# A chunked attention followed by a top-2 mixture of experts: tiles of 96 slots per pair of experts, the tokens beyond them in a list of each expert

## The chip, the cores and the metric

The kernel runs on one core of one Trainium2 chip, in one launch. A core has a matrix engine (TensorE, PE in the profile), three engines for vector work (VectorE or DVE, ScalarE or ACT, GpSimd or POOL) and SyncE (SP), which here only issues transfers. Each engine works through its own instructions in order; semaphores make one wait for another. Data lie in SBUF (128 partitions), matmul results in PSUM banks, inputs and outputs in DRAM. The metric is the device time of one execution in microseconds; smaller is better.

## The reference, cut to what matters

```python
def _attn_ref(q, k, v, mem_k, mem_v):              # (4, 8, 768, 64); chunks of 32, 16 to the left, 8 to the right, 8 memory rows
    ...
        a = np.exp(scores)
        a = a / (np.sum(a, axis=-1, keepdims=True) + 1e-09)
        out[:, :, c_start:c_end] = np.matmul(a, v_full)

def _moe_ref(x, w_gate, w_noise, noise, w1, w2):   # N=3072 tokens, D=512, E=8 experts, F=1024
    noisy_logits = x @ w_gate + np.log1p(np.exp(x @ w_noise)) * noise
    top2 = np.argpartition(-noisy_logits, 2, axis=1)[:, :2]
    ...
            h = np.maximum(x[mask] @ w1[e], 0.0)
            out[mask] += top2_w[mask, k, None] * (h @ w2[e])
```

Each token goes to the two experts with the largest noisy logits; their two outputs are added with the softmax of those two logits as weights. Inputs are drawn once, so the counts are the same in every run. Counted from that draw, a pair of experts has 87 to 135 tokens (28 pairs, 3072 tokens); one pair has more than 128, 23 have more than 96; the tokens beyond 96 of the seven pairs of an expert are 51 to 136.

## The kernel before, in words

The kernel has two stages. The first, to about 131 us, is the attention: 12 steps written out by hand (`ORDERS`), with the router's work in between. It writes the attention's rows to the DRAM tile `xd`, and routes each token to its **pair** of experts: `pcode` holds a code for each of the `NP` = 28 pairs, `ohp` is the one-hot of a token's pair, `rank` its place in it, `cum` the counts so far, `facts` five facts of a token besides (its row, its weights). One-hots of the rank (`oh_l`, L336) times these facts give, by matmul, `listed`: for each pair and each of 128 slots, which token stands there. From it come `main_src` (rows of `xd` to gather), `main_dst` (rows of the output) and `main_w` (weights).

The second stage runs the experts. The weights (float32 in DRAM, 2 MB for each of an expert's two layers) are cast to bf16 on their way into `w_all`, which holds all 8 experts, by transfers that POOL issues (L77, L79, L89, L91: `load_layer`, `load_part`). A pair's 128 rows are gathered by an indirect DMA of POOL (L896, `gather_x`), turned to columns by a DMA transpose of SP (L921) or, for the first six, by PE (L916), and lie in `xTs`, in blocks of 6 or 8 pairs. Twenty steps go through the blocks, an expert with 2, 3 or 4 of its pairs in each: `mm1` (L939) multiplies w1 by the columns into the banks `p_h`, ACT and DVE apply relu into `h` (L925, L927), `mm2` (L950) multiplies by w2 into `p_y`, of which there are two banks. A pair's first expert writes `y` (ACT, L954), its second adds to it (DVE, L956), and POOL puts the rows into the output (L902). The second layer of a step runs after the first layer of the next, so relu is not waited for. Tokens of a pair beyond 128 go to extra tiles: up to 32 of the first such tile through the spare tile in column groups of the array (L1122, L1142), with weights loaded for it anew (L1078, L1079); more by a branch at the end (L1220).

What sets the order: PE, ACT, DVE and SP are ordered by hand in the first stage, PE at the stage's start and otherwise by the scheduler's estimate; POOL's transfers are marked to keep the program's order (`pin`), but the scheduler's order can differ from the text's, as shown below. All transfers that POOL issues go into one queue, `q0`, SP's into `q1`.

## Time and profile before

| | |
|---|---|
| runs | 347.87, 348.86, 343.81 us; median 347.87 |
| span of the profiled execution | 344.8 us |
| PE busy | 291.0 us (84%) in 3332 matmuls |
| DVE, ACT, POOL busy | 157.4, 132.7, 150.9 us |
| transfers of POOL's queue | 40.51 MB, 60.9% of 16 DMA engines' span |
| transfers of SP's queue | 7.18 MB, 11.7% |

The profiled execution has no time of its own beside its span; the span lies inside the range of the runs, 3.1 us under their median. Busy times are sums over both stages, which have different limits, so they say little by themselves; the views below are read by stage. In the chain and in the timeline a row gives its start and its length in us, then engine, tile and line. `issue` is time in which an engine waited for nothing that the profile shows. In the list of transfers the last number is the median time from issue to landing.

### The profile page before, as it was taken

What the parts mean: (1) busy time and instruction counts of PE and PEld (TensorE: products, weight loads), DVE (VectorE), ACT (ScalarE), POOL (GpSimd) and SP (SyncE); (2) the same over time, 40 slices, a digit from 0 to 9 for tenths busy, and PEclk for the clock granted to TensorE, in tenths of its full rate; (3) what the DMA queues carried; (4) which work ended last, traced back from release to release, by engine and by line L of the source; (5) the groups of instructions that cost most, each with busy time, mean ns of one, the idle gap of its engine ahead of it and who ended that gap; (6) DMA issues with size and microseconds to landing.
All of it is one profiled execution on the core that took longest, in us unless ns stands there. A gap on an engine that the chain in (4) does not pass through costs nothing.

```text
span 344.8 us, 7971 instructions
## 1 busy us (share of the span) xinstructions
PE 291.0 (84%) x3332; PEld 192.8 (56%) x3332; DVE 157.4 (46%) x319; ACT 132.7 (38%) x220; POOL 150.9 (44%) x232
## 2 busy tenths in 40 slices
PE   0566889876778744999999999999999999999990
PEld 0465878765766633855544466664455775555550
DVE  4764657575579786311324166344310333312230
ACT  4656637553476310344231443213243222233300
POOL 4679678944019156821821555231670132201142
PEclk9969898888799655999999999999999999999997
DMA  7999959996804912897999999991289991100011
GB/s 123 212 211 194 222 104 209 189 179 114 161 2 72 201 33 62 134 205 195 172 194 207 267 138 249 199 167 54 92 167 189 204 209 59 55 2 2 27 73 58
DMA packets 41288, 48.32 MB, mean 140 GB/s; under 512 B 16000, under 2 KB 31362, under 8 KB 41244
## 3 DMA queue, kind: packets, MB, share of 16 engines
q0 software_dynamic: 23712, 40.51, 60.9%
q1 hardware_dynamic: 16988, 7.18, 11.7%
q8 instruction: 28, 0.46, 0.5%
q14 instruction: 16, 0.13, 0.1%
q10 hardware_dynamic: 544, 0.03, 0.1%
HBM read 64.88 MB, written 10.55 MB: 219 GB/s over the span
## 4 chain that ended last, share of the span: by engine, by line
PE 66%; DMA 5%; DVE 5%; issue 2%; ACT 2%; POOL 0%; POOLq 0%; SPq 0%; DVEq 0%
PE p_h L939 29%; PE p_y L950 28%; DMA w_all<-mvn 4%; PE p_t L409 2%; PE ps_o L578 1%; PE p_v L438 1%; DMA xt<-xd,main_src 1%; PE p_p L558 1%; PE p_xt L916 1%; ACT w_all L413 1%; ACT pT L564 1%; PE ps_s L465 1%; PE p_x L600 1%; DVE w_all L591 1%; PE p_rank L303 0%
## 5 line engine op out<-in xcount | busy, mean ns | idle before, releaser
L939 PE MATMUL p_h<-xTt,w_all 128*128 128x256 bf16 (+3 forms) x672 | 101.9, 312 | 0.5 <-DVE xTt L917 0.5
L950 PE MATMUL p_y<-w_all,h 128*128 128x512 bf16 x440 | 98.2, 379 | 0.0
L939 PEld LDWEIGHTS <-w_all 128*128 128x128 bf16 x672 | 65.3, 99 | 35.5 <-issue 0.9
L927 ACT ACTIVATE h<-p_h 128x512 bf16<-128x512 f32 (+1 forms) x79 | 43.4, 550 | 88.9 <-PE p_h L939 78.0
L950 PEld LDWEIGHTS <-h 128*128 128x128 bf16 x440 | 42.9, 98 | 49.2
L902 POOL DMA_INDIRECT out_dram<-y,main_dst x27 | 27.0, 998 | 82.4 <-DVE y L956 74.0
L925 DVE TENSOR_SCALAR h<-p_h 128x512 bf16<-128x512 f32 (+1 forms) x47 | 29.6, 631 | 69.0 <-PE p_h L939 63.4
L389 POOL COPY w_all<-w_all 128x512 bf16<-128x512 bf16 (+1 forms) x59 | 42.3, 785 | 17.1 <-PE p_t L409 11.8
L956 DVE SCALAR_TENSOR_TENSOR y<-p_y,main_w,y 128x512 f32<-128x512 f32 x27 | 20.3, 751 | 43.4 <-PE p_y L950 42.4
L896 POOL DMA_INDIRECT xt<-xd,main_src x28 | 27.4, 978 | 28.9 <-DMA xTt<-xt 12.1
L954 ACT ACTIVATE y<-p_y,main_w 128x512 f32<-128x512 f32 x28 | 19.2, 687 | 36.5 <-PE p_y L950 35.5
L409 PE MATMUL p_t<-identf,w_all 128*128 128x128 f32 x120 | 22.5, 337 | 0.4 <-ACT pT L564 0.4
L591 DVE TENSOR_TENSOR w_all<-ps_o,rs 128x512 bf16<-128x512 f32 x24 | 15.7, 683 | 7.3 <-PE ps_o L578 6.5
L409 PEld LDWEIGHTS p_t<-identf,w_all 128*128 128x128 f32 x120 | 17.9, 178 | 1.4 <-issue 1.0
L438 PE MATMUL p_v<-identf,w_all 128*128 128x128 f32 x96 | 15.9, 304 | 2.5 <-ACT w_all L413 1.8
L564 ACT COPY pT<-p_p 128x1024 bf16<-128x1024 bf16 x11 | 11.1, 1012 | 11.7 <-PE p_p L558 11.5
L478 DVE TENSOR_REDUCE mx<-ps_s 128x16 f32<-128x1024 f32 x12 | 14.7, 1223 | 1.8 <-PE ps_s L465 1.5
L480 DVE TENSOR_TENSOR w_all<-ps_s,mx 128x1024 f32<-128x1024 f32 x12 | 14.7, 1225 | 0.8
L551 ACT ACTIVATE pb<-w_all 128x1024 bf16<-128x1024 f32 x12 | 12.7, 1062 | 6.0 <-DVE w_all L480 6.0
L413 ACT COPY w_all<-p_v 128x512 f32<-128x512 f32 x21 | 11.9, 588 | 8.0 <-PE p_v L438 8.0
L578 PE MATMUL ps_o<-w_all,pT 64*32 64x64 bf16 x768 | 9.3, 201 | 6.6 <-DMA w_all<-mvn 4.4
L405 PE MATMUL p_t<-identb,w_all 128*128 128x128 bf16 x48 | 4.6, 270 | 11.9 <-DVE w_all L389 11.9
(220 smaller groups left out, 294.3 us busy)
## 6 DMA issues: line engine op xcount, KB each, us to landing
w_all<-in_moe_w_dram POOLq DMA_DIRECT2D x16, 1024.0 KB, 11.8
w_all<-in_moe_w_dram POOLq DMA_DIRECT2D x8, 512.0 KB, 12.7
w_all<-in_k_dram POOLq DMA_DIRECT2D x4, 768.0 KB, 11.5
w_all<-in_q_dram POOLq DMA_DIRECT2D x4, 768.0 KB, 9.2
w_all<-in_v_dram POOLq DMA_DIRECT2D x4, 768.0 KB, 12.4
xd<-w_all SPq DMA_DIRECT2D x24, 128.0 KB
w_all<-mvn SPq DMA_DIRECT2D x24, 32.0 KB
xt<-xd,main_src POOLq DMA_INDIRECT x28, 10.9
```

The costliest lines, as they stand in the source:

```text
L389: i = eng.tensor_copy(to, x)
L409: nc.tensor.transpose(out=p_t[:, s, :], in_=m.bitcast(F32)[:, s * 128:(s + 1) * 128], identity=identf)
L438: nc.tensor.transpose(out=p_v[:, i, c, :], in_=vT[:, c, c0:c0 + 128], identity=identf)
L591: nc.vector.tensor_tensor(out=xrow[b % 2][:, 2 * tp + j, 0:Dm].rearrange("p (x d) -> p x d", x=H), in0=ps_o[:, j], in1=bc(rs[:, :, j], D), ...
L896: i = nc.gpsimd.indirect_dma_start(out=xts[key].bitcast(I32), out_offset=None, in_=xd, in_offset=bass.IndirectOffsetOnAxis(ap=ix, axis=0))
L902: i = nc.gpsimd.indirect_dma_start(out=out if rows is None else rows, out_offset=bass.IndirectOffsetOnAxis(ap=ix, axis=0), in_=y, in_offse ...
L925: nc.vector.tensor_scalar(out=out_, in0=in_, scalar1=0.0, scalar2=None, op0=Alu.max)
L927: nc.scalar.activation(out=out_, in_=in_, func=Act.Relu)
L939: nc.tensor.matmul(out=o, lhsT=w(kp * F + f * 128, 128), rhs=x[:, kp], start=(kp == 0), stop=(kp == KP - 1))
L950: nc.tensor.matmul(out=p, lhsT=h[:, (f * n + j) * 128:(f * n + j + 1) * 128], rhs=w(KP * F + f * Dm, Dm), start=(f == 0), stop=(f == FB - 1))
L954: nc.scalar.activation(out=y, in_=p, func=Act.Copy, scale=weight)
L956: nc.vector.scalar_tensor_tensor(out=y, in0=p, scalar=weight, in1=y, op0=Alu.mult, op1=Alu.add)
```

## The change

A pair's tile has `MT` = 96 slots. The pairs are numbered anew: pairs (i, i+1), (i, i+2) and (i, i+3), counted around, are numbers 3i, 3i+1, 3i+2 (`out_of(i)` for expert i, `in_of` for the other one); the four **opposite** pairs (i, i+4) are numbers 24 to 27. Experts run one after the other. An expert has three tiles out, three in, one opposite pair of 96, and a list of its own with 160 places (`RS`): the tokens beyond 96 of its seven pairs, up to 64 of each (`RU`).

For the first layer an opposite pair's 96 columns and the 160 listed ones stand side by side in `x3`. For the second, a tile has 128 rows again: 96 of a pair and 32 beside them, from the opposite pair (tiles out, `hO`) or from the list's first 96 places (tiles in, `hI`); the list's last 64 places (`hB`) run in two column groups of 64. What the 32 rows give is copied by a second instruction on `p_y` into a unit tile (L1043).

The listed tokens' facts are made by one-hots once more (`rest_onehots`, `rest_list`), written to the DRAM tile `tdr`, and read back by indirect DMAs, two for each expert (`rest_facts`); decoded on DVE (`rest_decode`), gathered (`rest_rows`) and turned (`turn_rest`). A listed token is in the lists of both its experts: the earlier stores its weighted result to the output (`put_rest`), the later reads that back (`get_prev`, into `pA` and `pB`), adds its own and stores the sum. The spare tile is gone; a pair beyond 160 or a list beyond 160 goes to the branch at the end (`overflow`).

`w_all` keeps 5 experts (`WR`), expert e in place e % 5; what is freed holds `xs`, `hO`, `hI`, `hB` and `x3`. Weights are loaded in whole layers.

```diff
+    WR = 5
-            pin(nc.gpsimd.dma_start(out=w1v[:, e], in_=moe_w1[e].rearrange("(kp p) f -> p kp f", p=128)))
+            pin(nc.gpsimd.dma_start(out=w1v[:, e % WR], in_=moe_w1[e].rearrange("(kp p) f -> p kp f", p=128)))
...
-            eng.tensor_tensor(out=self.oh_l, in0=bc(self.rr, 128), in1=io_l.unsqueeze(1).to_broadcast([128, n, 128]), op=Alu.is_equal)
+            eng.tensor_tensor(out=self.oh_l, in0=bc(self.rr, MT), in1=io_l[:, 0:MT].unsqueeze(1).to_broadcast([128, n, MT]), op=Alu.is_equal)
...
+    def mm2_tiles(e, ps, h, unit):
+        for k, g in enumerate(ps):
+            p = psY.tile([128, Dm], F32, name="p_y")
+            for f in range(FB):
+                nc.tensor.matmul(out=p, lhsT=h[:, f, k, :], rhs=w2(e, f), start=(f == 0), stop=(f == FB - 1))
...
+                y = ys[g] = yp.tile([128, Dm], F32, name="y")
+                nc.scalar.activation(out=y[0:MT], in_=p[0:MT], func=Act.Copy, scale=wt)
+                keep_unit(0, unit[32 * k:32 * k + 32], p)
...
+    def ins_(e):
+        unit = yrp.tile([128, Dm], F32, name="yr")
+        mm2_tiles(e, in_of(e), hI, unit)
+        p = psY.tile([128, Dm], F32, name="p_y")[:, 0:Dm // 2]
+        for f in range(FB):
+            for g in range(2):
+                nc.tensor.matmul(out=p[g * RU:(g + 1) * RU], lhsT=hB[:, f, :], rhs=w2(e, f, g * Dm // 2, Dm // 2),
+                                 start=(f == 0), stop=(f == FB - 1), tile_position=(0, g * RU))
...
+            pA, pB = prev.pop(e)
+            nc.vector.scalar_tensor_tensor(out=yB, in0=p, scalar=wB, in1=pB, op0=Alu.mult, op1=Alu.add)
+            nc.vector.scalar_tensor_tensor(out=unit[0:MT], in0=unit[0:MT], scalar=wA, in1=pA[0:MT], op0=Alu.mult, op1=Alu.add)
+        put_rest(yB, dB, outB, 2 * N)
+        put_rest(unit[0:MT], dA, out, N)
+
+    def get_prev(e):
...
+        get_rest(pA[0:MT], rest_of[e][4], out, N)
+        get_rest(pB, rest_of[e][5], outB, 2 * N)
...
+    def rest_list():
...
+            nc.tensor.matmul(out=p, lhsT=oh_t[:, g], rhs=vals_t[:, g], start=(g == 0), stop=(g == NG - 1))
+        nc.vector.tensor_copy(tsb[:, :, 0:NV], p.rearrange("p v c -> p c v"))
+        for h in range(2):
+            nc.sync.dma_start(out=tdr.rearrange("(s h c) v -> h s (c v)", h=2, c=NC2)[h],
+                              in_=tsb[h * RU:(h + 1) * RU].rearrange("p c v -> p (c v)"))
+
+    def rest_facts(e):
+        for b, n in ((0, MT), (1, 128)):
+            i = nc.gpsimd.indirect_dma_start(out=fr[0:n, b, e], out_offset=None, in_=tdr,
+                                             in_offset=bass.IndirectOffsetOnAxis(ap=adr[0:n, b, e:e + 1], axis=0),
+                                             bounds_check=RU * NP - 1, oob_is_err=False)
+            pin(i)
...
+        mm1_main(0, in_of(0), hI, engs=(0,))
+        rest_list()
+        rest_facts(0)
+        rest_rows(0)
+        turn_rest(0)
+        rest_facts(1)
+        rest_rows(1)
+        turn_rest(1)
+        load_expert(3)
+        outs(0)
+        mm1_rest(1, r=False)
+        mm1_main(1, out_of(1), hO)
+        gather_main(QP + 2)
+        third = list(gathers(2))
+        load_expert(4)
+        mm1_rest(0, q=False)
...
+        outs(1)
+        ins_(0)
+        flush()
+        get_prev(1)
+        mm1_rest(1, q=False)
+        turn_q(2)
+        mm1_main(1, in_of(1), hI)
+        rest_facts(2)
+        rest_rows(2)
+        turn_rest(2)
...
+        load_expert(5)
+        ins_(1)
+        for e in range(2, E):
+            mm1_main(e, in_of(e), hI)
+            flush()
+            get_prev(e)
+            mm1_rest(e)
...
+            ins_(e)
+            if e + 4 < E:
+                load_expert(e + 4)
+            mm1_main(e, out_of(e), hO)
+            flush()
+            outs(e)
```

PE's work stands in the order of these lines. The other engines' instructions are moved by the scheduler. Two places of POOL's and one of DVE's follow; lines are those of the kernel they come from.

POOL before, at the start of the second stage, after the first six gathers (`xt` is a gathered tile, `w_all` the weights):

```order
L896 DMA xt<-xd,main_src 128x256 x6
L79 DMA w_all<-in_moe_w_dram 128x8x512
L77 DMA w_all<-in_moe_w_dram 128x4x1024
L79 DMA w_all<-in_moe_w_dram 128x8x512
L896 DMA xt<-xd,main_src 128x256 x8
```

Weights and gathers alternate there, and nothing is read that the stage itself wrote.

POOL in the changed kernel, after its first 13 gathers and one layer of weights. `fr<-tdr` are the reads of `rest_facts`; the first two rows here are the last two of eight, those of experts 0 to 3. `rs_3287` and `rs_3326` are the listed rows of experts 0 and 1:

```order
L1207 DMA fr<-tdr,adr 96x8
L1207 DMA fr<-tdr,adr 128x8
L934 DMA xt<-xd,rs_3287 96x256
L934 DMA xt<-xd,rs_3287 64x256
L934 DMA xt<-xd,rs_3326 96x256
L934 DMA xt<-xd,rs_3326 64x256
L79 DMA w_all<-in_moe_w_dram 128x4x1024
L81 DMA w_all<-in_moe_w_dram 128x8x512
L934 DMA xt<-xd,main_src 96x256 x5
```

The reads of experts 1, 2 and 3 have moved ahead of expert 0's row gathers, which the program's text has first.

POOL in the changed kernel, a little further on, after both layers of expert 4: row gathers of expert 2 (`rs_3779`), the weights of expert 5, the stores of expert 0's listed results (`yB`, `yr`) and the read-backs for expert 1 (`pA`, `pB`):

```order
L934 DMA xt<-xd,rs_3779 96x256
L934 DMA xt<-xd,rs_3779 64x256
L934 DMA xt<-xd,main_src 96x256 x4
L79 DMA w_all<-in_moe_w_dram 128x4x1024
L956 DMA out_dram<-yB,rd_3297 6144x256
L956 DMA out_dram<-yr,rd_3297 3072x512
L81 DMA w_all<-in_moe_w_dram 128x8x512
L965 DMA pA<-out_dram,ri_3340 96x512
L965 DMA pB<-out_dram,ri_3340 128x256
```

One layer of expert 5 has moved ahead of the stores and the other ahead of the read-backs; the text has the read-backs ahead of both.

DVE before, where the counts of the spare tile stand among the relus (L925) of the sixth step:

```order
L956 SCALAR_TENSOR_TENSOR y<-p_y,main_w,y 128x512 x3
L925 TENSOR_SCALAR h<-p_h 128x512 x3
L1020 COPY cnt<-p_xt 128x28
L1023 TENSOR_TENSOR scr<-cnt,kx 128x644
L1035 TENSOR_SCALAR over<-cnt 128x28
L1024 TENSOR_REDUCE ext<-scr 128x28
L925 TENSOR_SCALAR h<-p_h 128x512
```

DVE in the changed kernel at the end of expert 1's tiles in, where the read-back is added (L1096, L1097), with the first relus of expert 2 (L974) and the first decodes (`rt`, `rw`) behind:

```order
L1043 COPY yr<-p_y 32x512 x2
L1096 SCALAR_TENSOR_TENSOR yB<-p_y,rg_3338,pB 128x256
L1097 SCALAR_TENSOR_TENSOR yr<-yr,rg_3338,pA 96x512
L974 TENSOR_SCALAR w_all<-p_h 128x2x2x96
L1104 MEMSET pA 128x512
L974 TENSOR_SCALAR w_all<-p_h 128x2x2x96
L1105 MEMSET pB 128x256
L1218 TENSOR_TENSOR rt_4341<-fr 128x2
L1234 TENSOR_TENSOR rw_4359<-fr 128x2
L1218 TENSOR_TENSOR rt_4647<-fr 128x2
```

Before, what DVE adds in this stage lies in SBUF or PSUM; now two of its instructions take what a transfer brings, and the relus of the next expert stand behind them.

745 lines of the change are left out of this document (437 added, 308 removed).

## The prediction

> **What bounds the kernel now.** I read three views in this order: the page's 40 slices, stretches of the span with the busy time of each engine, and the chain that ended last. A stretch's row gives its length, then the busy time of PE, weight load, DVE, ACT and POOL, then granted clock, DMA share and GB/s.
>
> ```profile
> PE   0566889876778744999999999999999999999990
> PEclk9969898888799655999999999999999999999997
> DMA  7999959996804912897999999991289991100011
> ...
> 135.70:336.30 200.60, 200.24 (x1273) 113.88 (x1272) 64.69 (x131) 64.03 (x112) 68.85 (x73) 0.99 0.74 141
> 336.30:344.80 8.50, 0.00 (x0) 0.00 (x0) 0.44 (x1) 0.00 (x0) 2.06 (x3) 0.75 0.17 59
> ```
>
> From 135.7 us the expert stage runs, and PE is busy 200.24 of 200.60 us: nothing else sets the time there, and any new gap in PE is paid in full. 8.5 us follow PE's last matmul. The chain prices the work (start, us, engine, tile, line, matmuls):
>
> ```profile
> 135.74 1.87 PE p_h L939 x16
> ...
> 159.47 5.18 PE p_y L950 x24
> 164.65 5.20 PE p_h L939 x32
> ...
> 175.03 6.91 PE p_h L939 x32
> ...
> 225.25 3.49 PE p_h L939 x32
> ...
> 296.87 0.99 PE p_h L1122 x32
> ```
>
> One expert's first layer is 32 matmuls: 3.49 us at 256 columns, 5.20 at 384, 6.91 at 512. So a matmul of N columns takes 2.3 + 0.4175 N ns at full clock. A second-layer tile (8 of 512) takes 1.73 us. L1122 shows column groups: 32 matmuls of 256 columns in four groups of the array take 0.99, not 3.49, so groups run together.
>
> **PE's work.** Per expert the changed kernel streams 3+3 tiles of 96 slots, one opposite pair of 96 and 160 listed columns, 832 where 7 x 128 = 896 stood. By the formula: 288 columns 3.92 us, 256 3.49, 192 2.64, 160 2.21, 96 1.36. Second layer: six tiles 10.36, and the 64-row rest in two column groups, between 0.87 (8 x 109 ns, together) and 1.74 (in turn); I take 1.0, nearest to L1122. Experts 3 to 7: 3.92 x 2 + 3.49 + 10.36 + 1.0 = 22.69 each; 2, 1 and 0 (split runs): 22.77, 22.85, 22.85. With 24 matmuls of 84 columns for the list (0.9) and 16 transposes (0.7) the sum is 183.6 us. Before it is 200.6, the spare tile included. So 17 us of PE work go. This is the gain; the rest is what it costs.
>
> **Front of the stage.** The 96-slot one-hots save about 0.5 us on DVE ahead of the first gather. But DVE's order puts L1194 (2016 elements) before the first transposed copy.
>
> ```profile
> L343 DVE TENSOR_TENSOR vals_last<-ohp,facts 128x448 bf16<-128x448 bf16 x1 | 0.6, 626 | 0.0
> ...
> L1065 DVE TENSOR_TENSOR scr<-kt,io_s 128x3072 bf16<-128x3072 f32 x1 | 3.3, 3348 | 0.0
> ...
> 138.00:139.00 1.00, 1.00 (x12) 1.00 (x10) 0.50 (x1) 0.24 (x1) 0.83 (x1) 0.50 0.36 94
> 139.00:140.00 1.00, 1.00 (x15) 0.96 (x14) 0.42 (x2) 0.00 (x0) 1.00 (x2) 0.94 0.34 90
> ```
>
> At 626 ns for 448 elements it is 2.75 us; against its place in before, PE starts at 136.8, 1.1 later. The clock stands at 0.50 until PE has worked 3.3 us without a gap (135.74 to about 139.06), so the first 96-column layer takes 2.7. Then transposes 0.9, DVE copies 1.0, 192 columns 3.5 (part at half clock), transposes and an ACT copy 0.8, 1.36, 3.92, the list 0.9: the list ends at 151.9. L1192's 3.35 us of DVE (as L1065) lies inside that. From there 172.7 us of PE work remain: with no wait PE ends at 324.6, where before it ends at 336.3. POOL's larger tables at about 65 us I cost at nothing, because POOL waits 4.8 us for PE soon after; bare they are up to 2.
>
> **Wait A: the first listed rows.** PE's order after the list is three second-layer tiles, 96 and 288 columns of expert 1 (5.18 + 1.36 + 3.92 = 10.5 us of cover, to 162.4), then expert 0's 160 listed columns. These need: list to DRAM, eight indirect reads (POOL's order has those of experts 0 to 3 before the first row gather), two gathers, two DMA transposes.
>
> ```profile
> 245.51 1.01 POOL L896 DMA_INDIRECT xt<-xd,main_src  x1 [0.30 <-issue]
> 246.82 0.99 POOL L896 DMA_INDIRECT xt<-xd,main_src  x1 [0.30 <-issue]
> ...
> xt<-xd,main_src POOLq DMA_INDIRECT x6, 3.1
> out_dram<-y,main_dst POOLq DMA_INDIRECT x2, 2.7
> ...
> 111.81 7.58 DMA w_all<-mvn
> ...
> 248.46 9.77 SPq L921 DMA_TRANSPOSE xTt<-xt  x6
> ...
> L993 DVE COPY xTt<-xTt x1: 294/294/294, 252.8 to 252.8; 128x512 bf16<-128x512 bf16 x1
> ```
>
> An indirect DMA holds POOL for 1.28 us and lands 2.7 to 3.1 us later when nothing is ahead; a transpose issued at 248.46 released its reader at 252.8, 4.2 later. The write to DRAM isn't in the trace: 2.7 (a put in an empty queue) to 7.6 (L448's under load); I take 3, since one load is then about to land. 151.9 + 0.3 + 3 + 8 x 1.28 + 1.28 + 3.0 + 4.2 = 173.9. PE waits 11.5 us (7 to 17, by the bounds of the write and 3 us for a transpose).
>
> ```profile
> 113.00:114.00 1.00, 0.77 (x20) 0.77 (x18) 0.90 (x2) 0.00 (x0) 0.02 (x1) 1.00 1.11 195
> 114.00:115.00 1.00, 0.02 (x1) 0.02 (x1) 1.00 (x3) 0.21 (x1) 0.00 (x0) 1.00 1.16 223
> ...
> 116.00:117.00 1.00, 1.00 (x44) 0.94 (x29) 0.71 (x2) 0.38 (x2) 0.00 (x0) 0.50 1.02 223
> ```
>
> Two microseconds of little work were enough for the clock to fall to 0.50, and it comes back after 3.3: 1.65 lost at each long gap. **13.2 us.**
>
> **Wait B: the result read back.** POOL's order from here: row gathers of expert 1 (to 170.5), expert 3's weights, 5 gathers, expert 4's weights, 6 gathers, w1 of expert 5, the two stores of expert 0's listed results, w2 of expert 5, and the two read-backs for expert 1, which wait for the stores to land. What stands behind weights in that queue waits for them:
>
> ```profile
> 164.82 0.86 POOL L77 DMA_DIRECT2D w_all<-in_moe_w_dram  x1
> ...
> 168.56 1.06 POOL L902 DMA_INDIRECT out_dram<-y,main_dst  x1 [0.30 <-issue]
> ...
> out_dram<-y,main_dst POOLq DMA_INDIRECT x1, 24.3
> ...
> w_all<-in_moe_w_dram POOLq DMA_DIRECT2D x16, 1024.0 KB, 11.8
> ```
>
> Four layers were issued from 164.82; the put behind them landed 24.3 us after 168.56, at 192.9. That is 28 us, 7.0 a layer (5.9 by the last row, if its layers went in pairs). Six layers (42) and the small transfers between (11 gathers and two stores; a gather has 98 KB where a layer writes 1024 and reads twice that, so 0.3 to 0.7 us, I take 0.5: 6.5) put the read-back at 170.5 + 48.5, about 219.5 with its own landing. On DVE L1096, which adds it, stands ahead of the relus of expert 2, and all of DVE waits behind it. PE by then: 173.9 + 1.65 + 2.21 + 5.18 + 6.18 + 2.21 + 4.00 + 6.18 = 201.5; it runs 3.3 us of expert 2 and stops at 204.8, when its banks are full of p_h that DVE hasn't read. DVE needs
>
> ```profile
> L968 DVE SCALAR_TENSOR_TENSOR y<-p_y,main_w,y x2: 484/484/484, 335.2 to 336.3; 128x256 f32<-128x256 f32 x2
> L956 DVE SCALAR_TENSOR_TENSOR y<-p_y,main_w,y x27: 750/751/752, 164.8 to 334.4; 128x512 f32<-128x512 f32 x27
> ...
> 203.48 0.14 DVE L1030 COPY inc<-ext 128x1 f32<-128x1 f32 x1
> ...
> 205.01 0.15 DVE L1036 COPY over<-inc 128x1 f32<-128x1 f32 x1
> ```
>
> 0.48 + 0.75 + 0.4: PE goes on at 221.2, a wait of 16.4, and 1.65 of clock. Queued behind on DVE are 55 small decodes of experts 4 to 7 (11 such steps, 203.48 to 205.01, took 1.53 us: 0.14 each, 8 us) among the relus that expert 2's second layer needs; PE covers about half: 4.5. **22.6 us** (11 with 5.9 a layer and the decodes hidden, 30 with all of them bare and 4 us more for the stores). The spare tile's accumulate, late before, has no successor.
>
> The Trainium skill, DMA: Bandwidth & Descriptors, section "Anatomy of one DMA", gives about 2.0 us + bytes / 436 GB/s for a transfer, by which a read-back of 196 KB takes about 2.5 us (an estimate from that page), and wait B would be nothing and the sum about 23 us less. The same page's "Queues, rings and completion order" says that descriptors of a ring are consumed in ring order; the 24.3 us row agrees with that section and not with the formula alone.
>
> **Later experts.** The read-backs for experts 3 and 4 stand behind two layers (14 us), issued at the end of the listed results; 16.5 us of PE work (3.92 + 5.18 + 3.92 + 3.49) and 6.18 more stand before they are needed. Hidden, with some 4 us to spare; uncovered they cost that difference. POOL issues 118 indirect DMAs for 59 (151 us at 1.28, in 225), SP 44 transposes for 23: free outside A and B, where the experts' periods of 22.7 us hold 13 x 1.28. Each p_y now has two readers in turn, 0.69 or 0.75 and about 0.69; with two banks that just fits in 1.73. I take 2 us in all, of 0 to 14 (48 tiles, each late by half a DVE step of 0.6).
>
> **The end.** Two more DVE steps and a put follow PE's last tile: 0.5 on 8.5.
>
> **Sum.** 324.6 + 13.2 + 22.6 + 2 + 9.0 = 371.4 us of span, for 344.8. The median of the three runs, 347.87, is 3.1 above this span, so about **374 us**, 7.6% slower. Its own range: 357 (A, B and p_y at their low ends) to 390 (A and p_y high, which is most of the way to all three).
>
> **Rivals.** *Only A remains*: the read-backs pass the weights (queue not in order). For: most puts land in 2.7. Against: 24.3. It gives 374.4 - 22.6 = 352. *On the other side, PE's sum decides*: the small transfers are fast enough to stay under PE. Its place is the eight reads: 32 bytes a row, which may hold POOL for far less than gathers of 1 KB a row; were they and the landings 11.5 us shorter, A is gone, and if the read-back comes before 203, B. Then 324.6 + 2 + 9.0 + 3.1 = 339, or 337 without p_y: 2.6 to 3.2% faster. Against: the before row's 1.28 does not look like it goes with bytes (puts of 2 KB a row take the same 0.98 as gathers of 1 KB). *More than A and B*: the read-backs behind experts 6's and 7's weights or the two readers of p_y stop PE every expert: two waits of 5 and 10 of p_y, 392. *Not what it says*: a pair over 160 tokens or an expert over 160 listed would enter the long branch at the end; counted from the reference's draw the largest are 135 and 136, so hardly.
>
> **Chances.** Forecast 0.63, more than that 0.15, only A 0.12, PE's sum 0.09, the branch 0.01. Two per cent is about what a measurement of this kernel tells from no change: 341 to 355. Slower 0.79, same 0.12, faster 0.09. The range that leaves out 0.09 below and some 0.09 above: 346 to 390.
>
> **What would show it.** In the profile after: PE's gap of about 11 us before the 160-column matmuls of L988, released by DMA; a DVE wait of 15 to 20 us at L1096 released by pB, and PE's gap after it; 22.7 us an expert from expert 3 on; no long wait after. Wrong if L1207's issues are much shorter than 1.28, or a read-back lands in 3 us with weights ahead of it.

## The result: slower by 14%, just outside the range, and the profile after

| | before | after |
|---|---|---|
| runs | 343.81 to 348.86 us, median 346.65 of 4 | 392.29 to 397.69 us, median 393.89 of 4 |
| ratio | | 1.1391, interval 1.1302 to 1.1481 |
| span of the profiled execution | 344.8 us | 391.8 us |

The forecast was 374 us with a range of 346 to 390. The direction and the chance for "slower" held; the time is 19.9 us above the forecast and 3.9 outside the range.

The 40 slices of the changed kernel, rows as before. Of the expert stage, slices 14 and 15 (127 to 147 us), 18 and 19 (167 to 186) and 23 to 26 (215 to 255) are the poor ones; from slice 27 to the tail PE is busy.

```profile
PE   0487798768875409953989267699999999999950
PEclk9888989889965557965999758899999999999995
DMA  7999699994381159007999911497995031123220
```

Stretches of the same execution, with columns as in the prediction (length, then PE, weight load, DVE, ACT, POOL, then granted clock, DMA share, GB/s). They are cut at PE's first matmul of the stage, the end of the list's matmuls, the waits and PE's end:

```profile
131.10:159.60 28.50, 15.84 (x184) 14.40 (x184) 10.30 (x44) 7.71 (x18) 11.97 (x13) 0.69 0.59 110
159.60:192.10 32.50, 20.67 (x137) 12.37 (x135) 12.51 (x87) 6.55 (x17) 19.93 (x21) 0.74 0.50 84
192.10:218.00 25.90, 24.32 (x233) 16.48 (x232) 10.07 (x19) 8.88 (x17) 9.48 (x10) 1.00 1.18 209
218.00:255.05 37.05, 20.96 (x120) 11.98 (x120) 15.87 (x96) 5.81 (x17) 24.49 (x25) 0.72 0.47 89
255.05:376.98 121.93, 120.33 (x826) 75.89 (x823) 60.11 (x124) 45.29 (x103) 52.77 (x57) 1.00 0.47 103
376.98:391.80 14.82, 0.18 (x1) 0.00 (x0) 1.50 (x2) 0.58 (x1) 3.59 (x4) 0.63 0.20 58
```

The list's matmuls end at 159.6, where 151.9 was forecast, PE at 377.0 instead of 362.4, and the tail is 14.8 instead of 9.0. The first of these was in no step and no rival of the prediction. PE's rows there (start, length, work, idle time before it and its releaser), and below them four rows of the waits by releaser (total, times, longest):

```profile
134.95 0.62 PE L1126 MATMUL p_xt<-identb,xt 96*128 96x96 bf16 x8
147.03 5.28 PE L988 MATMUL p_h<-w_all 128*128 128x192 bf16 x32 [11.46 <-issue]
...
228.30 7.16 PE L988 MATMUL p_h<-w_all 128*128 128x96 bf16 x48 [10.35 <-DVE w_all L974]
...
ACT w_all L976 <- remote: 18.9, 4, 7.4
...
DVE w_all L1127 <- remote: 10.1, 2, 5.3
...
DVE w_all L974 <- remote: 4.8, 1, 4.8
...
DVE yB L1096 <- remote: 3.6, 1, 3.6
```

"Remote" is a wait for a semaphore whose releaser no row shows. PE's transposes end at 135.57; DVE's copies of them (L1127) wait 10.1 us in two parts. In the trace's semaphore events, the update of PE that releases the last of these copies stands at 146.60, 11.0 us after the end of the matmul record it belongs to. Between 139 and 252 us, 18 updates stand over 0.9 us behind the last record that ended before them. The trace also lacks events: 336 of PE's 355 updates and 407 of DVE's 505 are there, and so many of the transfers' updates are missing that the views give no landing time. I call this **held completions**; before's profile has none. The experiments had to separate it from what the program does.

### The profile page after: what moved, and what is told of

Same layout as the page of the kernel before. It is cut to its first block, busy times and chain, and to the rows that moved or that the text cites. A ratio compares the mean times of both kernels' runs of the same rounds, so it can differ in the third digit from the quotient of the medians.

```text
span 391.8 us, 8903 instructions
## 1 busy us (share of the span) xinstructions
PE 290.9 (74%) x3550; PEld 207.9 (53%) x3550; DVE 202.9 (52%) x551; ACT 143.4 (37%) x281; POOL 203.0 (52%) x291
## 5 line engine op out<-in xcount | busy, mean ns | idle before, releaser
L988 PE MATMUL p_h<-w_all 128*128 128x288 bf16 (+4 forms) x928 | 107.4, 280 | 40.2 <-issue 21.7
L988 PEld LDWEIGHTS <-w_all 128*128 128x128 bf16 x928 | 85.6, 105 | 61.5 <-issue 44.5
L1049 PE MATMUL p_y<-w_all 128*128 128x512 bf16 x384 | 88.1, 384 | 3.5 <-ACT w_all L976 3.0
L976 ACT ACTIVATE w_all<-p_h 128x288 bf16<-128x288 f32 (+3 forms) x115 | 43.0, 380 | 125.0 <-PE p_h L988 79.8
L1049 PEld LDWEIGHTS <-w_all 128*128 128x128 bf16 x384 | 36.8, 98 | 49.5 <-ACT w_all L976 4.9
L974 DVE TENSOR_SCALAR w_all<-p_h 128x288 bf16<-128x288 f32 (+3 forms) x99 | 38.9, 404 | 42.2 <-PE p_h L988 30.5
L1058 DVE SCALAR_TENSOR_TENSOR y<-p_y,main_w,y 96x512 f32<-96x512 f32 x24 | 17.9, 747 | 20.7 <-PE p_y L1049 17.9
L1207 POOL DMA_INDIRECT fr<-tdr,adr x16 | 15.9, 995 | 22.0 <-ACT y L1054 17.4
L1054 ACT ACTIVATE y<-p_y,main_w 96x512 f32<-96x512 f32 x24 | 16.4, 682 | 24.7 <-PE p_y L1049 22.1
L1043 ACT COPY yr<-p_y 32x512 f32<-32x512 f32 x24 | 13.9, 578 | 30.8 <-DVE y L1058 25.4
L934 POOL DMA_INDIRECT xt<-xd,rs x16 | 14.8, 925 | 13.5 <-issue 10.2
L458 PE MATMUL p_v<-identf,w_all 128*128 128x128 f32 x96 | 15.9, 305 | 2.8 <-ACT w_all L433 1.8
L1043 DVE COPY yr<-p_y 32x512 f32<-32x512 f32 x12 | 8.3, 694 | 16.8 <-ACT y L1054 16.8
L429 PEld LDWEIGHTS p_t<-identf,w_all 128*128 128x128 f32 x120 | 15.2, 158 | 2.4 <-issue 1.3
```

Source lines behind the costliest of these rows:

```text
L429: nc.tensor.transpose(out=p_t[:, s, :], in_=m.bitcast(F32)[:, s * 128:(s + 1) * 128], identity=identf)
L458: nc.tensor.transpose(out=p_v[:, i, c, :], in_=vT[:, c, c0:c0 + 128], identity=identf)
L934: pin(nc.gpsimd.indirect_dma_start(out=t[0:n].bitcast(I32), out_offset=None, in_=src_, in_offset=bass.IndirectOffsetOnAxis(ap=ix, axis=0)))
L974: nc.vector.tensor_scalar(out=out_, in0=in_, scalar1=0.0, scalar2=None, op0=Alu.max)
L976: nc.scalar.activation(out=out_, in_=in_, func=Act.Relu)
L988: nc.tensor.matmul(out=o if len(xk.shape) == 2 else o.rearrange("p (j t) -> p j t", j=xk.shape[1]), lhsT=w_all[:, e % WR, kp * F + f * 128 ...
```

## Experiments

Theory W (waits of the program): the missing time is in the steps of the prediction, mis-sized: the list's way to the rows, the read-back, the end. Theory H (held completions): something in the changed program makes PE's updates arrive late, and that is where the missing time is. The expectations number the theories anew for each kernel.

The 18 kernels ran in five sets, one profiled execution each. In the first two sets (e_tail, e_poolorder, e_g128, b_split; e_facts, e_pause, e_noback, e_noif), all eight profiled executions show held completions, and before had 348.11 and 347.61 us. In the last three (the other ten kernels), none does, and before had 343.15, 343.7 and 343.25. The first two sets ran on two chips and the last three on two others, so the chip differs wherever the held completions do; the chip of the first result is not known. Ratios are to before of the same set.

### Is it the form of the program?

**e_g128**: gathers of 128 rows instead of 96.

```diff
-        xt[g] = gather("xt", xd, src[0:MT, g:g + 1], MT, xqp if g >= QP else None)
+        xt[g] = gather("xt", xd, src[:, g:g + 1], 128, xqp if g >= QP else None)
```

> The changed kernel with row gathers of 128 rows for the pairs (the 32 rows more are row 0 and are not used). In the changed kernel DVE and ACT start 4 to 11 us after PE's recorded end between 135 and 147 us, while POOL issues 13 gathers of 96 rows in a row. Theory 1 (the form of 96 rows is what delays PE's completions): the gap of 11.5 us before the 192 columns is gone, 1 to 2 us are left, and the span falls by some 10 us to 380 to 384. Theory 2 (an unbroken row of indirect DMAs delays them, whatever their rows): the gap stays at 9 to 13 us and the span at 389 to 395.

390.61 us (one run). The gap was 8.33, a little under theory 2's 9 to 13, and the updates were late: the gather's form is not the cause.

**e_pause**: POOL is stopped behind its fourth gather until the 192-column relu is done.

```diff
+        gap = late.tile([128, 16], BF16, name="gap")
+        pin(nc.gpsimd.tensor_copy(gap, hO[:, FB - 1, 1, 0:16]))
+        first_in = list(gathers(0))
```

> The changed kernel with POOL stopped behind its fourth row gather until the relu of the 192 columns of expert 0 is done; the other nine gathers of that row come then. Theory 1 (PE's completions are held while POOL issues its unbroken row of 13): PE's gap of 11.5 us ahead of the 192 columns falls to 0.5 to 3 us, DVE and ACT start behind PE's recorded ends there without a wait, the list's matmuls end at 146 to 151 us instead of 159.6; the stall may come back where the nine gathers stand now. Theory 2 (the gap comes from the transposes on PE or from something else at that place): the gap stays at 9 to 13 us. The span: 380 to 392, for the rows of expert 1 come later.

397.28 us (one run). The gap ahead of the 192 columns fell from 11.46 to 1.10, and the moved gathers were then waited for, so the list's matmuls still ended at 157.9 and nothing was gained:

```profile
137.88 2.80 PE L988 MATMUL p_h<-w_all 128*128 128x192 bf16 x32 [1.10 <-DVE w_all L1127]
...
150.32 4.69 PE L988 MATMUL p_h<-w_all 128*128 128x288 bf16 x24 [7.18 <-DMA w_all<-xt]
```

In this execution the late updates moved with POOL's row of indirect transfers (the moved gathers are issued from 142.0 to 152.8, and the first update over 1 us late stands at 146.5). No second run repeats it.

**b_split, b_split4, b_space**: the kernel before, with first-layer matmuls of 384 and 512 columns cut in two (128 and 256, and 256 and 256), all of them cut to 128 columns, and the cut in two with a memset of the target ahead of each gather behind the first twelve, so that the gathers don't stand in an unbroken row.

```diff
+                cut = [(0, n)] if n < 3 else [(0, n // 2), (n // 2, n)]
+                for j0, j1 in cut:
```

> The kernel before, with its first-layer matmuls of 384 and 512 columns cut in two halves of 192 and 256; nothing else moves. By the fit of the prediction (2.3 ns for each further matmul) PE's work grows by some 4 us. Theory 1 (PE's completions are held during a row of indirect DMAs on POOL when PE runs many matmuls of few columns, as in the changed kernel; before, 384 and 512 columns kept PE under that rate): PE's semaphores come late by over 0.3 us in the rows of gathers at 142 to 149, 196 to 205 and 242 to 254 us, DVE and ACT wait there, and the span is 354 to 375. Theory 2 (the count of matmuls has nothing to do with it): no such lateness, and the span is 347 to 351.

> The kernel before, with every first-layer matmul cut to 128 columns; nothing else moves. Theory 1 (a row of indirect DMAs on POOL holds PE's completions, the more the more matmuls PE runs in that time): PE's completions come later than with 192 and 256 columns, where the longest lateness was 2.4 us and PE lost 3.5 us at 252.6; here PE waits 8 to 30 us in all at the rows of gathers, and nothing where POOL issues none. Time 362 to 390, of which up to 10 us for the matmuls themselves (2.3 ns each). Theory 2 (the count of matmuls has no part in it): no lateness over 0.5 us and PE's gaps as in the kernel before; 351 to 358.

> The kernel before with first-layer matmuls of 192 and 256 columns, and ahead of each row gather behind the first twelve a memset of its tile on POOL, so that the gathers no longer stand in an unbroken row. Theory 1 (the unbroken row is what holds PE): the lateness of 2.4 us at 254 to 255 and PE's gap of 3.5 us at 252.6 are gone or under 1 us, and the time is 346 to 350. Theory 1b (each indirect DMA holds PE for its part, spaced or not): lateness and gap stay at 2 to 4 us and the time at 350 to 354.

b_split, in the first set: 351.05 (one run), updates up to 2.4 us late. So the kernel before, with this cut, can have them too, though far less. b_split4, in the third set: 348.9, ratio 1.0180 (1.0146 to 1.0214), and b_space 343.78, 1.0047 (1.0005 to 1.0089): none late. In that set the changed kernel has none either (next run), so these two don't show whether the count of matmuls or the unbroken row has a part where updates are late at all; they show that neither makes them late by itself.

**a_again**: the changed kernel, unchanged, in that third set.

> The changed kernel once more, beside these on one chip. If the held completions belong to the program, PE's gap ahead of the 192 columns is again 8 to 14 us, DVE and ACT start late in the same three places (135 to 147, 165 to 185 and 246 to 251 us), and the time is 390 to 398; if they were chance of one execution, the gaps move or are gone and the time is under 385.

385.33 us (382.93, 387.72), ratio 1.1243 (1.1074 to 1.1412), span 381.0, no late update. The place where 11.46 us stood:

```profile
135.62 0.84 PE L1126 MATMUL p_xt<-identb,xt 96*128 96x96 bf16 x8
136.98 3.10 PE L988 MATMUL p_h<-w_all 128*128 128x192 bf16 x32 [0.52 <-DVE w_all L1127]
```

The same text, other timing: the program by itself doesn't hold the updates, so theory H as it stands falls. Whether the program sets how late they come is open: b_split's came at most 2.4 us late, those of the seven changed kernels in the first two sets 5.6 to 14.2. Three texts ran both with and without held completions: 393.89 and 385.33 us, and two below 408.21 and 393.65, 397.98 and 384.34. With them the changed kernel took 9 to 15 us more, and before, by its medians in the sets, about 4; since the chips differ too, what of this the held completions cost was not separated. The intervals of the two ratios of the changed kernel overlap, those of the second pair (1.1673 to 1.1873, and 1.1353 to 1.1506) do not. What holds the updates stays open. The chip is one candidate. That trace events go missing in the same executions suggests recording as another; neither was tried.

### What the program itself does: a_again read by the prediction's steps

POOL and SP around the list, and PE's waits (a_again):

```profile
148.44 0.99 POOL L81 DMA_DIRECT2D w_all<-in_moe_w_dram  x1
161.21 1.03 POOL L1207 DMA_INDIRECT fr<-tdr,adr  x1 [11.78 <-DMA tdr<-tsb]
...
170.32 1.00 POOL L1207 DMA_INDIRECT fr<-tdr,adr  x1 [0.30 <-issue]
171.63 0.93 POOL L934 DMA_INDIRECT xt<-xd,rs  x1 [0.31 <-PE p_h L988]
...
153.36 1.14 SPq L1202 DMA_DIRECT2D tdr<-tsb  x2
174.84 5.38 SPq L1258 DMA_TRANSPOSE w_all<-xt  x4
...
149.76 1.09 PE L1199 MATMUL p_xt<-w_all 128*128 128x84 bf16 x24
...
169.38 4.96 PE L988 MATMUL p_h<-w_all 128*128 128x288 bf16 x20 [10.52 <-DVE w_all L974]
181.12 4.42 PE L988 MATMUL p_h<-w_all 128*128 128x160 bf16 x32 [6.78 <-DMA w_all<-xt]
...
226.68 5.81 PE L988 MATMUL p_h<-w_all 128*128 128x96 bf16 x48 [13.86 <-DVE w_all L974]
...
DVE yB L1096 <- DMA pB<-out_dram,ri: 17.7, 2, 15.2
...
DVE rt L1218 <- DMA fr<-tdr,adr: 12.4, 3, 9.0
```

Wait A is there in two parts. DVE stands in its order at the list's decodes ahead of expert 1's relus, so PE stops first with full banks (10.52), then for the rows (6.78): 17.3 for a forecast of 11.5. Wait B is there as forecast, at L1096 by pB: 13.86 for 16.4. From the issue of the first of its six layers (176.23) to the read-back's landing (224.91 by the semaphore events) 48.7 us pass, where the forecast had about 49.

### Single moves

**e_write**: w2 of expert 2 is loaded behind the list's reads of expert 1 instead of ahead of the list.

```diff
-    load_layer(2, 1)
...
+        load_layer(2, 1)
         load_expert(3)
```

> The load of expert 2's second layer is issued behind the list's reads of expert 1 instead of ahead of the list. Compared with the same execution (span 381.0, the list's first write issued 153.36 and the read that waits for it at 161.21, so 7.3 us from the second write's issue at 153.91). Theory 1 (the write takes that long because a 2 MB load issued 148.44 holds the DMA engines): the read follows 2.5 to 4.5 us after the write's issue, wait A 3 to 5 us shorter, span 366 to 378. Theory 2 (a write to DRAM and its completion take 7 us by themselves, the load has no part): 6.5 to 8 us again, span 379 to 384, or more where expert 2's second layer then comes late.

```profile
152.30 1.61 SPq L1202 DMA_DIRECT2D tdr<-tsb  x2
...
156.04 0.98 POOL L1207 DMA_INDIRECT fr<-tdr,adr  x1 [9.50 <-ACT y L1054]
```

The read follows 2.1 us after SP's row ends (153.91), in a_again 6.7 (154.50 to 161.21): the 1 MB layer ahead of the write cost 4.6 us. The other executions without held completions agree: 2.1 in all four that load this layer behind the list's reads, 6.7 to 7.3 in all four that load it ahead. In these four the semaphore events show the layer landing (159.74 in a_again) and the write landing 0.2 to 0.7 us behind it (159.98 to 160.39), although the write is in SP's queue and the layer in POOL's. (The row of e_write names ACT's L1054, which ended at about the same time; in both kernels the read is issued 0.8 us behind the write's last update, 155.24 and 160.39.) So theory 1 is right on the write, and wait A fell to 4.30 + 6.26. But the time is 390.3, ratio 1.1374 (1.1296 to 1.1452), span 388.3 where 366 to 378 was expected: nothing was gained.

**e_facts, e_facts2** (one text, with and without held completions): the list reads of experts 1 to 7 wait until expert 0's list is decoded. **e_comb** has both edits.

```diff
-                                             in_offset=bass.IndirectOffsetOnAxis(ap=adr[0:n, b, e:e + 1], axis=0),
+                                             in_offset=bass.IndirectOffsetOnAxis(ap=(adr2 if e else adr)[0:n, b, e:e + 1], axis=0),
```

> The changed kernel with the list reads of experts 1 to 7 made to wait for expert 0's decoded list (their addresses are copied with a zero multiple of it added). On POOL the two row gathers of expert 0 then follow two list reads instead of eight, and the stores of expert 0's result and the read-backs for expert 1 come ahead of expert 5's weights, behind four layers instead of six. Theory 1 (the order on POOL sets waits A and B): PE's 160 listed columns start 5 to 8 us earlier against the end of the list's matmuls (26.3 us in the changed kernel, 18 to 21 here), PE's gap of 10.4 us ahead of expert 2 falls to 0 to 5, and the span is 374 to 383. Theory 2 (held completions, not order): the distance from the list to the 160 columns stays at 24 to 28 and the span at 387 to 396.

> The list reads of experts 1 to 7 are made to wait for expert 0's decoded list, so POOL issues expert 0's two row gathers behind two list reads instead of eight. Compared with the changed kernel's execution in which PE's semaphore updates were on time (span 381.0 us, ratio 1.124, rows of expert 0 issued at 171.63, wait B 13.86). Theory 1 (six reads of 1.31 us sit on the path of wait A, in POOL's order, and the rest of the chain follows): rows at 166 to 167, the 160-column matmuls of L988 4 to 6 us sooner, all that is queued behind on POOL sooner by as much, wait B 0 to 9, span 362 to 374, ratio 1.07 to 1.10. Theory 2 (the path only moves): the later list reads now stand behind weights in the queue and DVE's decodes (L1218) wait for them, span 374 to 384, ratio 1.10 to 1.135. If semaphore updates come late again in this execution, span 395 or more, and the run says nothing on the two.

> Both edits together. Theory 1: both shorten wait A by their own parts (5 and 3 to 4 us) and wait B follows POOL, span 356 to 370, ratio 1.045 to 1.09. Theory 2: neither or only one is on the path, span 374 to 384.

408.21 us, 1.1773 (1.1673 to 1.1873); 393.65, 1.1429 (1.1353 to 1.1506); 392.4, 1.1439 (1.1349 to 1.1529). e_facts, with held completions, has a span of 405.4, above both its theories. Theory 1 of the two later runs falls. Theory 2 has the direction, with spans (393.3 and 389.9) above its numbers: wait A was shorter, and the later waits grew by more (the table below).

**e_poolorder**: POOL's transfers in the text's order. **e_noback**: nothing is read back (the earlier expert's part of the listed tokens is left out). **e_noback2**: the same, and all list reads are issued ahead of expert 3's weights (in the changed kernel those of experts 4 to 7 stand behind expert 5's).

```diff
-    with tc.manual_schedule(engines={ET.PE}):
+    with tc.manual_schedule(engines={ET.PE, ET.Pool}):
...
-        get_prev(1)
...
+        for e in range(2, E):
+            rest_facts(e)
```

> The changed kernel with POOL's DMAs in the order in which they are written: expert 0's two list reads, its two row gathers, expert 1's two reads and gathers, the weights of experts 3 and 4, then the stores of expert 0's result and the read-backs for expert 1, and only then the reads of expert 2 and the weights of expert 5. Theory 1 (waits A and B come from the order on POOL's queue): rows of expert 0 are asked for some 7 us earlier and PE's 160 listed columns come 5 to 8 us before the 185.9 us of the changed kernel; the read-back stands behind four layers instead of six and PE's gap of 10.4 us at 218 falls to 0 to 4; span 374 to 383. Theory 2 (PE's results come late because its completions are held while POOL issues indirect DMAs in an unbroken row; order matters little): the lateness of PE's semaphores moves but its sum stays, and the span stays at 386 to 394.

> The changed kernel without the read-backs: each expert's listed result is stored as it is, and what an earlier expert stored there is not added, so listed rows of two experts hold one part only. Theory 1 (wait B is the read-back behind the weights in POOL's queue): PE's gap of 10.4 us ahead of expert 2's 96 columns falls under 1 us, DVE's wait of 11.7 us at L1096 is gone, and the span falls by 12 to 20 us, to 372 to 380. Theory 2 (something else, such as DVE's decodes or the lists of experts 4 to 7, stops PE there): the gap stays over 5 us and the span at 383 to 392.

> The changed kernel without the read-backs (an earlier expert's stored result is not added), and with the list reads of experts 4 to 7 brought up behind the row gathers of expert 1, ahead of expert 3's weights. Without the read-backs alone PE still stopped 15.3 us at 214.7, for DVE's decode of a later expert's list waited from 214 to 229 us for a read that stood behind weights. Theory 1 (whatever small transfer DVE waits for behind weights stops PE there; the read-back was one, the list read the next): the gap at 214 falls under 3 us and PE's end comes 10 us sooner than without the read-backs alone (383.4); the 8 reads more in the row hold expert 3's weights up by 10 us, which nobody waits for. Span 380 to 390. Theory 2 (another cause): a gap over 6 us stays between 205 and 235 us.

422.32 us, 1.2140 (1.2015 to 1.2265): wait A was shorter, but each expert's list reads now stood behind weights, and DVE waited for them 49.0 us in six places. e_noback: 400.76, 1.1543 (1.1408 to 1.1678), above both its theories. Without a read-back, wait B stayed, by another transfer of the same queue:

```profile
230.00 1.92 PE L1087 MATMUL p_y<-w_all 128*64 128x256 bf16 x16 [15.31 <-DVE rw L1234]
...
DVE rt L1218 <- DMA fr<-tdr,adr: 21.5, 4, 17.0
```

e_noback2: 377.39, 1.1011 (1.0944 to 1.1078), span 374.7. At B 6.15 and 5.32 are left, now for the transposes of rows: the gap named by theory 1 is gone, and one over 6 us stays, as theory 2 has it. This is the fastest of all, with part of the work left out; its distance from e_noback is not the edit's alone, for that one ran with held completions.

### All moves at once

**e_order**: e_write's edit, with all list reads ahead of these weights; expert 5's weights then stand behind the read-back for expert 1. **e_order_noif**: the same without the branch.

```diff
-    load_layer(2, 1)
...
+        for e in range(2, E):
+            rest_facts(e)
+        load_layer(2, 1)
         load_expert(3)
```

> Only the order of POOL's transfers is another: the list reads of experts 2 to 7 are issued ahead of expert 3's weights, expert 2's second layer behind them, and expert 5's weights behind the read-back for expert 1. Theory 1 (the waits are the price of small transfers that stand behind 1 or 2 MB layers in POOL's queue, and of nothing else): against e_write (span 388.3, PE gaps of 4.30 and 6.26 at wait A, 3.86, 4.24, 12.98 and 6.49 at wait B) the last two gaps go, since no list read lands behind expert 5's weights; the others stay: span 366 to 373, ratio 1.07 to 1.095. Theory 2 (the queue has a fixed amount to carry between 150 and 250 us, and whatever is moved, something else comes last): a new gap of 10 us or more appears, most likely at the transposes of expert 2's rows, span 378 to 390, ratio 1.11 to 1.14.

> The same, without the overflow branch (no token of these inputs needs it). Theory 1: 2.5 to 3.5 us less than e_order, as between the changed kernel (tail of 15.1 us) and e_noif2 (tail of 12.0): span 363 to 370, ratio 1.06 to 1.085, still slower than before. Theory 2: 375 to 387.

387.15 us, 1.1240 (1.1151 to 1.1329), and 384.72, 1.1194 (1.1093 to 1.1295). Theory 2 holds. POOL's and SP's rows of e_order show why:

```profile
185.18 0.99 POOL L81 DMA_DIRECT2D w_all<-in_moe_w_dram  x1
186.12 0.85 POOL L79 DMA_DIRECT2D w_all<-in_moe_w_dram  x1
186.89 0.97 POOL L81 DMA_DIRECT2D w_all<-in_moe_w_dram  x1
188.16 1.01 POOL L934 DMA_INDIRECT xt<-xd,main_src  x1 [0.30 <-issue]
...
208.41 0.98 POOL L956 DMA_INDIRECT out_dram<-yr,rd  x1 [0.30 <-issue]
221.00 1.01 POOL L965 DMA_INDIRECT pA<-out_dram,ri  x1 [11.60 <-issue]
...
206.92 5.18 SPq L1116 DMA_TRANSPOSE w_all<-xt  x4
...
220.67 1.46 PE L988 MATMUL p_h<-w_all 128*128 128x96 bf16 x16 [11.21 <-DMA w_all<-xt]
```

Three layers are issued from 185.18; the gathers behind them, issued from 188.16, are turned only from 206.92 (19 us), and PE waits 11.21. The put issued at 208.41 stands behind expert 4's weights, and POOL waits 11.60 for it before the read-back. PE's idle times over 0.25 us after the list, read from such rows in the eight runs of the changed kernel without held completions:

| run | wait A | B, to 255 us | sum | us |
|---|---|---|---|---|
| a_again | 17.3 | 15.6 | 32.9 | 385.3 |
| e_noif2 | 15.3 | 15.9 | 31.2 | 384.3 |
| e_facts2 | 11.4 | 23.1 | 34.6 | 393.7 |
| e_write | 10.6 | 27.6 | 38.1 | 390.3 |
| e_comb | 9.9 | 26.1 | 36.0 | 392.4 |
| e_order | 9.6 | 26.2 | 35.8 | 387.2 |
| e_order_noif | 8.7 | 26.6 | 35.3 | 384.7 |
| e_noback2 | 14.5 | 11.5 | 26.0 | 377.4 |

What A loses, B gains. (Spans of single executions say less: PE's first expert matmul stands between 131.2 and 137.3 us in them, though the text of the first stage is the same. From there to PE's end it is 232.8 us in a_again, 234.7 in e_noif2 and 241 to 244 in the five rows below them with the whole work.) The layers of experts 2 to 5 have to pass POOL's queue in this time. DMA's share by stretches, first two rows a_again, last three e_order:

```profile
150.85:185.34 34.49, 17.18 (x120) 11.77 (x119) 11.42 (x79) 5.67 (x15) 19.02 (x20) 0.65 0.59 88
185.34:212.81 27.47, 27.47 (x250) 18.10 (x249) 11.50 (x26) 9.89 (x20) 10.43 (x11) 1.00 1.20 195
...
155.00:170.00 15.00, 10.90 (x98) 6.84 (x97) 6.29 (x37) 4.03 (x9) 7.96 (x8) 0.87 0.09 13
170.00:185.00 15.00, 10.22 (x61) 6.74 (x61) 8.87 (x87) 3.90 (x12) 11.50 (x12) 0.79 0.22 46
...
200.00:215.00 15.00, 9.41 (x84) 6.01 (x82) 2.59 (x4) 3.42 (x6) 2.97 (x3) 0.96 1.18 215
```

Keeping the queue clear for the list leaves the DMA engines at 0.09 to 0.22 for 30 us, and the layers that were not carried then are in the way afterwards. No order of one queue tried here serves both.

### The end

**e_tail**: the last stores are issued ahead of the branch, and its flag is made to depend on the last result. **e_noif, e_noif2**: no branch.

```diff
-        nov = nc.values_load(nxt[0:1, 0:1], min_val=0, max_val=E * (E + 1),
...
-        with tc.If(nov > 0):
-            overflow()
...
+    flush()
```

> The changed kernel with its last puts ahead of the branch at the end, and the branch's flag made to depend on the last result, so that DVE's last accumulate (L1076) stands ahead of the branch on DVE. Theory 1 (the accumulate waited for the branch): in the changed kernel DVE's branch stands from 377.99 to 381.06 us and L1076 starts at 381.17, 4.2 us behind PE's last matmul (376.98); ahead of the branch it starts about 0.3 us behind ACT's copy, the last put goes 3 us earlier, and the span falls by 3 to 6 us, to 386 to 389; the stretch behind PE's last matmul falls from 14.8 to 9 to 12 us. Theory 2 (the closing drain of POOL, 8.99 us for 7.11, sets the end whatever stands ahead of it): the stretch stays within 1.5 us of 14.8 and the span at 390 to 393. What lies ahead of PE's last matmul doesn't change by either.

> The changed kernel without the branch for pairs and experts that are too large (it isn't entered with these data); the last puts stand at the end. Theory 1 (DVE's last accumulate and POOL's last put stand behind the branch): the stretch behind PE's last matmul falls from 14.8 us to 8.5 to 11, and the span to 385 to 389. Theory 2 (POOL's closing drain follows the last put by a fixed 9 us and the branch lies beside it): the stretch stays at 13 to 15 us.

> The changed kernel without the overflow branch at the end (no token of these inputs needs it, so the output is whole). Compared with span 381.0, of which 15.1 us follow PE's last record. Theory 1 (the branch ahead of DVE's last accumulate costs 3 to 4 us of the tail): tail 11 to 12.5, span 376 to 379. Theory 2 (the tail is the chain of last accumulate, put and queue drain, and the branch is hidden): tail 14.5 to 15.5, span 380 to 382.

e_tail: 402.89 us, 1.1590 (1.1479 to 1.1701), a tail of 19.0. Both theories missed: the last put is issued at 388.78, and POOL's closing wait starts only at 396.63, behind the branch. e_noif, with held completions: 397.98 (394.81 to 401.15), with the same tail of 12.0 as e_noif2. e_noif2: 384.34, 1.1186 (1.1083 to 1.1288); the tail is 12.0 against a_again's 15.1 (theory 1; its span of 376 to 379 didn't come, 383.5, for PE's first expert matmul stood 3.7 later than in a_again), and 6.6 in e_order_noif against 9.7 in e_order. So the branch is 3.1 us of the tail, twice. DVE's rows at the branch of a_again say where:

```profile
L1445 DVEq COMPARE_BRANCH  x1: 72/72/72, 366.8 to 366.8; - x1
...
L1445 DVEq EVENT_SEMAPHORE  x1: 21/21/21, 370.3 to 370.3; - x1
...
370.38 0.75 DVE L1076 SCALAR_TENSOR_TENSOR yq<-yr,main_w,yq 96x512 f32<-96x512 f32 x1 [3.66 <-DVEq L1445]
```

The last accumulate, L1076, stands behind DVE's part of the branch and waits 3.66 us for it. By medians these 3.1 us are within the intervals of the totals.

## Why the prediction missed, by its own steps

The forecast has PE's first expert matmul at 136.8, PE's end 225.6 us later (362.4) and a tail of 9.0, in all 371.4. The profiled execution starts there at 132.4, runs 244.6 to PE's end and has a tail of 14.8; a_again starts at 133.1, runs 232.8 and has 15.1. So two steps failed in both, the clock's share of PE's work and the end. In the profiled execution the front failed too: the list was to end at 151.9 and ended at 159.6, because of the wait of 11.46 us that stood in no step. In a_again it is wait A instead.

The write that feeds wait A is another one in the two executions. In the profiled one the list came so late that the layer ahead of it had landed (156.0 by the semaphore events), and the read followed 2.1 us after SP's row:

```profile
160.06 1.62 SPq L1202 DMA_DIRECT2D tdr<-tsb  x2
...
163.83 1.03 POOL L1207 DMA_INDIRECT fr<-tdr,adr  x1 [17.41 <-ACT y L1054]
```

There PE's gaps from the list to the end of the listed columns add up to 11.8 us, for 11.5 forecast, but that is luck: none of them was released by the rows' transposes, and two of ACT's relus among them wait 10.7 us for late updates ("remote").

The sum over the stretches of a_again from 131.77 us on, in the columns of before (length, PE, weight load, DVE, ACT, POOL):

```profile
sum 249.23, PE 194.86 PEld 129.46 DVE 110.97 ACT 75.83 POOL 124.09; mean PE 32.48 PEld 21.58 DVE 18.50 ACT 12.64 POOL 20.68
```

- **"So 17 us of PE work go", and "1.65 lost at each long gap"**: the matmuls did go, but PE's busy time fell less: it is 194.86 us in a_again, 202.29 in the profiled execution, for 183.6 of work at full clock and 200.24 in before. The 11 and 19 us are mostly work at a lower clock (0.85, 0.65 and 0.82 in a_again's stretches with waits), for which the forecast had 1.65 at each of two gaps and some 2 at the front. The mechanism was right, its size too small: work that is spread between waits stays at half clock (from 170 to 185 us a_again has 8.22 us of work, all at 0.50, and the 160 columns took 4.42, not 2.21).
- **Front**: PE began at 133.10, not 136.8; the order of L1194 was right (it takes 2.25 us, not 2.75), but the first gather stood at 128.34 where before's is at 131.72, more than the 0.5 of the shorter one-hots. This hid 3.7 of the other errors by luck, for PE's start varies from 131.2 to 137.3 between executions.
- **Wait A, "I take 3" for the write**: this step failed in a_again. The write's way from the end of SP's issue to the read was 6.7 us with the layer ahead of it and 2.1 without (e_write, and the profiled execution). I had the bound of 7.6 and set it aside with "one load is then about to land"; the load was there, but it had been issued at 148.44, 4.9 us before the write, and landed only at 159.74. SP adds 2.5 us between the last matmul at 150.85 and the issue at 153.36, for which I had 0.3: its row of five transposes ends at 153.19. Eight reads, gathers and transposes took 19.9 (161.21 to 181.12), 18.7 forecast. In all 17.3 for 11.5.
- **Wait B**: mechanism right (15.2 us at L1096 by pB), and PE's gap 13.86 for 16.4. The 7.0 us a layer, the row it came from and the ring order that the Trainium skill states (DMA: Bandwidth & Descriptors, "Queues, rings and completion order") stand: e_order's gathers wait about 19 us behind three layers. The formula in the section "Anatomy of one DMA" of the same page of the Trainium skill, about 2.0 us + bytes / 436 GB/s, gives 2.0 us for a list read of 4 KB (an estimate from that page). The list reads with nothing ahead of them landed in 2.3; behind weights the formula is not the time.
- **"Hidden" later experts and p_y's two readers**: right. From 255 us PE is busy 120.33 of 121.93.
- **"The end ... 0.5 on 8.5"**: this step failed; a_again has 15.1. The branch is 3.1 of it. The closing wait of POOL's queue was 7.11 us in before, 8.99 in after, a_again and e_noif2, 3.61 in e_order; that is all of the 5.4 between the tails of a_again and e_order (15.1 and 9.7). Why it differs was not settled.
- **What was in no step**: held completions. The medians of the changed kernel with and without them are 8.6 us apart (393.89 and 385.33, the latter of two runs); before is 3.5 apart between the same two sets (346.65 and 343.15), so not all of the 8.6 need be theirs.

Of the 19.9 us, then, 11.3 are terms mis-sized (385.33 for 374), and 8.6 lie between runs with held completions and runs without. 385.33 lies inside the range, though wait A, the clock and the end were too small there as well. None of the rivals came true: the eight reads did hold POOL for 1.3 us each, and no read-back passed the weights. "More than A and B" has 392, near the measured 393.9, but by number only: no wait comes with every later expert.

A version that beats before was not found: the fastest whole results are e_noif2 and e_order_noif, 384 us. Weights through another queue than the gathers', and a list that doesn't go through DRAM, were not tried.

## What to carry to other kernels

Where data go through DRAM in the middle of a stage that streams weights, price the trip with the transfers that are in the queue and beside it, not with an empty queue: here 2.1 us became 6.7 to 7.3 for a write, although it was in another queue than the weights, and 3.1 became 19 for a gather behind three layers. When small transfers and weights share one queue, ask how much the queue has to carry in the whole stretch before moving anything: here four orders took 6 to 8 us from one wait, and the next one grew by 8 to 12. And 17 us of matmul work saved in the bounding engine were worth nothing here, since they brought two dependent round trips that the engine stood still for, and it also worked at half clock around them.

## What had not been expected of the hardware

PE's semaphore updates arriving up to 14 us after the end of their records (11 in the profiled execution above), in whole sets of runs (all eight executions of two sets, none of ten in three, on other chips), with trace events missing in the same executions and with the kernel before 1.3% slower there as well (348 against 343.4). A small write to DRAM from SP's queue was seen by a reader after 2.1 us, or after 6.7 to 7.3 where a 1 MB layer in POOL's queue was still on its way, and then 0.2 to 0.7 us behind that layer. And a branch that is not taken held DVE for 3.7 us.
